# Two x tiles turned by DMA instead of on TensorE, and the k and v loads moved behind them, in a fused attention and GEGLU kernel

## The chip, the cores and the metric

The kernel runs on one core of a Trainium2 chip. The metric is the device time of one execution in microseconds (us), the median of several runs. Before the change it is 325.5 us (three runs, 325.27 to 325.55).

A core has TensorE (PE, matrix products), VectorE (DVE), ScalarE (ACT), GpSimd (POOL) and SyncE (SP), which here only issues transfers. The engines run beside each other, each works through its own instructions in program order, and they wait for one another through semaphores. The data lie in on-chip memory (SBUF); TensorE writes its results to a second memory (PSUM) of eight banks. Sixteen DMA engines move data between HBM and SBUF.

## The reference, cut to what matters

```python
# q, k, v: (8 batches, 8 heads, 576 positions, 64)
def phi(x, c, s):                       # c, s: cos and sin of the position
    r = np.maximum(x, 0.0)
    return np.concatenate([r * c, r * s], axis=-1)
q_p, k_p = phi(q, cos_w, sin_w), phi(k, cos_w, sin_w)
kv  = np.einsum('bhsf,bhsd->bhfd', k_p, v)
z   = np.sum(k_p, axis=2)
num = np.einsum('bhsf,bhfd->bhsd', q_p, kv)
den = np.einsum('bhsf,bhf->bhs', q_p, z)[..., None] + 1e-06
x   = (num / den).transpose(0, 2, 1, 3).reshape(4608, 512)

g    = x @ w_gate                       # 512 x 1536
gelu = 0.5 * g * (1.0 + erf(g / sqrt(2)))
out  = (gelu * (x @ w_val)) @ w_out     # 1536 x 512
```

Linear attention is followed by a gated feed-forward layer. Attention makes x with the tokens along the partitions; the products `x @ w_gate` and `x @ w_val` need x with its features along the partitions. Each 128 x 512 tile of x must therefore be turned. Where and when two of these tiles are turned is what the change is about.

## The kernel before

A batch has 576 tokens: four tiles of 128 and one of 64. The feed-forward layer works on blocks of tokens: block 0 is batch 0 (576 tokens), block 1 is the next 512 tokens, which are tiles 0 to 3 of batch 1, and so on. A unit (`gv_unit`) makes 128 of the 1536 hidden features of one block: four matmuls for the gate, a gelu on ScalarE, four matmuls for the value, and the product of both on VectorE. Gate results alternate between PSUM banks 0 and 1, value results between 2 and 3.

```python
def gate(n, jt, c0, w, gb, ct0=0, ct1=CT):          # TensorE, then ScalarE
    for ct in range(ct0, ct1):
        nc.tensor.matmul(ps[:, gb, 0:w], lhsT=wg_sb[:, ct, jt * 128:(jt + 1) * 128],
                         rhs=xT[:, ct, p0:p0 + w], ...)         # L232
    nc.scalar.activation(gel[:, 0:w], ps[:, gb, 0:w], AF.Gelu)  # L239
# value(): the same with wv_sb (L245), then product() on VectorE (L254)
```

The next block's attention is woven between these units. q and k are loaded as float32, scaled to bf16 by `sq` and `sk` on VectorE ("v", L136) or ScalarE ("s", L138), and v is cast to bf16:

```python
def cast_v(b, h0, h1, eng="v"):                      # L142
    cp(vx[b % 2][:, :, h0:h1, 0:D], vf[:, h0:h1].rearrange("p h j d -> p j h d"))

def kv_half(b, g, bank, eng="s", heads=None):        # 20 matmuls, L155, read kp and vx
def numer_mm(b, t, bank, g, rows=128):               # 4 matmuls, L171, read qT and kv
def norm(xb, bank, g0, g1, rows=128):                # VectorE: den, rec, then xb (L186)
```

A finished tile of x (`xb`) is turned in one of two ways. By DMA, from SyncE's queue:

```python
def turn_x(b, t, xb):
    p0 = b * S + t * 128
    xb2 = xb.rearrange("p g h d -> p (g h d)")
    if t < NJ:
        nc.sync.dma_start_transpose(out=xT[:, :, p0:p0 + 128], in_=xb2)   # L219
    ...
```

or by TensorE, with a copy from PSUM by ScalarE or VectorE:

```python
def x_by_pe(b, t, xb, bank, eng, c0=0, c1=CT):
    for ct in range(c0, c1):
        nc.tensor.transpose(out=view[:, ct, 0:rows], in_=xb2[...], identity=ident[...])  # L362
    if eng is not None:
        x_evac(b, t, bank, eng, c0, c1)              # one copy to xT, L373
```

Between block 0 and block 1 the output matmuls of block 0 (`o_part`, twelve a tile, L279; the last of them is followed by a copy on ScalarE, L309, and a store from SyncE, L311) are mixed with batch 1's attention:

```python
o_tile(0, 0, 4)
sk(NJ, 1, "s")
load_k(2)
cast_v(1, 0, 4, "v")
...
load_v(2)
o_part(0, 1, 5, 0, 6)
kv_half(1, 0, 6, "s")
kv_half(1, 1, 7, "v")
o_part(0, 1, 5, 6, 12)
y = [new_xb() for _ in range(4)]
for g in (0, 1):
    numer_mm(1, 0, 0, g)
    numer_mm(1, 1, 2, g)
norm(y[0], 0, 0, 2)
norm(y[1], 2, 0, 2)
o_part(0, 2, 4, 0, 6)
...                                  # numerator and norm of tile 2
x_by_pe(1, 0, y[0], 0, "s")
o_part(0, 2, 4, 6, 10)
x_by_pe(1, 1, y[1], 1, "s")
...                                  # numerator and norm of tile 3
o_part(0, 2, 4, 10, 12)
o_part(0, 3, 5, 0, 2)
x_by_pe(1, 2, y[2], 6, "s")
o_part(0, 3, 5, 2, 7)
x_by_pe(1, 3, y[3], 7, "s")
o_part(0, 3, 5, 7, 12)
for j in range(NJ + 1):
    sq(j, 0, "v")
sq(0, 1, "s")
```

Block 1 then starts with its units 0 to 11. For block n, `put(u, ...)` appends work behind unit u, with b = n + 1 and s = -1 for block 1 (0 for the later ones):

```python
put(2 + s, L(sk, 0, 0, "v"), L(sk, 1, 0, "v"), L(sk, 0, 1, "s"), L(sk, 1, 1, "s"))
put(3 + s, L(sk, 2, 0, "v"), L(sk, 3, 0, "v"), L(sk, 4, 0, "v"))
put(3 + s, L(sk, 2, 1, "s"), L(sk, 3, 1, "s"), L(sk, 4, 1, "s"), L(cast_v, b, 0, 4))
put(4 + s, L(cast_v, b, 4, 8, "s"))
put(5 + s, L(attn_step, b, 0))       # the two kv_half of batch b
```

Of the kernel before, what the change touches and what calls it, by code (L numbers as in the profile page):

```python
# [16 lines left out]
def kernel(  # L17
# [59 lines left out]
    def load(dst, t, b, h0=0, h1=H, even=None, odd=None, j0=0, j1=NJ + 1):  # L77
        runs = t[b, h0:h1].rearrange("h (i r) d -> i h r d", r=9)
        for s, r0, n, eng in ((1, 5, 4, odd), (0, 0, 5, even)):
            n = min(n, j1)  # L80
            (eng or nc.sync).dma_start(
                out=dst[s:128:2, h0:h1, j0:n].rearrange("p h j d -> p h (j d)"),
                in_=runs[:, :, r0 + j0:r0 + n].rearrange("i h r d -> i h (r d)"),
            )
# [55 lines left out]
    def cast_v(b, h0, h1, eng="v"):  # L140
        cp = nc.vector.tensor_copy if eng == "v" else nc.scalar.copy
        cp(vx[b % 2][:, :, h0:h1, 0:D], vf[:, h0:h1].rearrange("p h j d -> p j h d"))  # L142
# [35 lines left out]
    def norm(xb, bank, g0, g1, rows=128):  # L178

        n = g1 - g0  # L180
        nd = ps[0:rows, bank + g0:bank + g1, 0:4 * (D + 1)].rearrange("p g (h e) -> p g h e", e=D + 1)
        den = rot.tile([128, 2, 4], FP32, name="den")
        nc.vector.tensor_scalar(den[0:rows, 0:n], nd[:, :, :, D], EPS, None, op0=ALU.add)  # L183
        rec = rot.tile([128, 2, 4], FP32, name="rec")
        nc.vector.reciprocal(rec[0:rows, 0:n], den[0:rows, 0:n])
        nc.vector.tensor_tensor(  # L186
            xb[0:rows, g0:g1], nd[:, :, :, 0:D],
            rec[0:rows, 0:n, :, None].to_broadcast([rows, n, 4, D]), op=ALU.mult,
        )
# [14 lines left out]
    def new_xb():  # L204
        return rot.tile([128, 2, 4, D], BF16, name="xb", bufs=4)
# [9 lines left out]
# [5 lines that stand above are left out]
        else:  # L220
            xr = rot.tile([128, CT, 128], BF16, name="xr")
            nc.sync.dma_start_transpose(out=xr, in_=xb2)
            nc.gpsimd.tensor_copy(xT[:, :, p0:p0 + 64], xr[:, :, 0:128:2])  # L223
# [52 lines left out]
    def o_part(n, m, bank, j0, j1):  # L276
        c0 = 128 * m - starts[n] + 64
        for jt in range(j0, j1):
            nc.tensor.matmul(  # L279
                ps[:, bank, :], lhsT=hT[n % 2][:, jt, c0:c0 + 128], rhs=wo_sb[:, jt, :],  # L280
                start=(jt == 0), stop=(jt == JT - 1),
            )
        if j1 == JT:
            o_store(m, bank)
# [47 lines left out]
    def load_k(b):  # L332
        load(kf, k, b)

    def load_v(b):
        load(vf, v, b)
# [20 lines left out]
    def x_by_pe(b, t, xb, bank, eng, c0=0, c1=CT):  # L357
        xb2 = xb.rearrange("p g h d -> p (g h d)")
        rows = 128 if t < NJ else 64
        view = ps[:, bank, 0:256].bitcast(BF16).rearrange("p (c t) -> p c t", c=CT)  # L360
        for ct in range(c0, c1):
            nc.tensor.transpose(  # L362
                out=view[:, ct, 0:rows], in_=xb2[0:rows, ct * 128:(ct + 1) * 128], identity=ident[0:rows, 0:rows],
            )
        if eng is not None:
            x_evac(b, t, bank, eng, c0, c1)

    def x_evac(b, t, bank, eng, c0=0, c1=CT):
        p0 = b * S + t * 128
        cp = nc.vector.tensor_copy if eng == "v" else nc.scalar.copy  # L370
        rows = 128 if t < NJ else 64
        view = ps[:, bank, 0:256].bitcast(BF16).rearrange("p (c t) -> p c t", c=CT)
        cp(xT[:, c0:c1, p0:p0 + rows], view[:, c0:c1, 0:rows])  # L373
# [4 lines left out]
    def sk(j, which, eng, *h):  # L378
        scale(K, j, which, eng, *h)
# [110 lines left out]
    def L(f, *a):  # L490
        return lambda: f(*a)
# [24 lines left out]
        sk(j, 1, "s")  # L516
    o_tile(0, 0, 4)
    sk(NJ, 1, "s")
    load_k(2)
    cast_v(1, 0, 4, "v")  # L520
    cast_v(1, 4, 6, "v")
    cast_v(1, 6, 8, "s")
    load_v(2)
    o_part(0, 1, 5, 0, 6)
    kv_half(1, 0, 6, "s")
    kv_half(1, 1, 7, "v")
# [1 line left out]
    y = [new_xb() for _ in range(4)]  # L528
# [6 lines left out]
    for g in (0, 1):  # L535
        numer_mm(1, 2, 6, g)
    norm(y[2], 6, 0, 2)
    x_by_pe(1, 0, y[0], 0, "s")
    o_part(0, 2, 4, 6, 10)
    x_by_pe(1, 1, y[1], 1, "s")  # L540
    for g in (0, 1):
        numer_mm(1, 3, 2, g)
    norm(y[3], 2, 0, 2)
# [25 lines left out]
    for n in range(1, 7):  # L569
        b = n + 1  # L570
        a = after[n]

        def put(u, *fs):
            a[u].extend(fs)

        s = 0 if n > 1 else -1
        if n > 1:
            put(0, L(sq, 0, 0, "v"), L(sq, 1, 0, "v"), L(sq, 1, 1, "v"), L(sq, 0, 1, "s"))
            put(1, L(sq, 2, 0, "v"), L(sq, 2, 1, "s"), L(turn_q, b, 0, 3))
            put(1, L(sq, 3, 0, "v"), L(sq, 4, 0, "v"), L(sq, 4, 1, "v"), L(sq, 3, 1, "s"), L(turn_q, b, 3, 5))  # L580
        else:
            put(0, L(sq, 1, 1, "s"), L(sq, 2, 1, "v"), L(turn_q, b, 0, 3))
            put(0, L(sq, 3, 1, "v"), L(sq, 4, 1, "s"), L(turn_q, b, 3, 5))
        put(2 + s, L(sk, 0, 0, "v"), L(sk, 1, 0, "v"), L(sk, 0, 1, "s"), L(sk, 1, 1, "s"))
        put(3 + s, L(sk, 2, 0, "v"), L(sk, 3, 0, "v"), L(sk, 4, 0, "v"))
        put(3 + s, L(sk, 2, 1, "s"), L(sk, 3, 1, "s"), L(sk, 4, 1, "s"), L(cast_v, b, 0, 4))
        put(4 + s, L(cast_v, b, 4, 8, "s"))
        put(5 + s, L(attn_step, b, 0))
        if b + 1 < B:

            for f, u in zip((load_q, load_k, load_v), (3, 4, 5) if n > 1 else (1, 10, 11)):
                put(u, L(f, b + 1))
        for i in range(5):

            where = mid[n][6 + s + i] if n > 1 or i else after[n][5]
            where.append(L(attn_step, b, i + 1, 6 if n > 1 or i % 2 == 0 else 4))
# [50 lines left out]
```

## Time and profile before

| | |
|---|---|
| time, median of 3 | 325.5 us |
| span of the profiled execution | 325.0 us |
| TensorE busy | 314.3 us, 97% of the span |
| VectorE busy | 167.2 us, 51% |
| ScalarE busy | 151.9 us, 47% |
| DMA | 55.56 MB, 171 GB/s on average |
| granted TensorE clock | 0.995 of full speed |
| block 1's first gate starts on the chain | 59.67 us |
| kv of batch 2 starts on the chain | 68.30 us |

The profile lists for each engine how long it was busy. The chain of work that ended last is followed back from the last instruction, at each step to what released it; a gain or a loss on this chain is one of the whole run. The timeline lists instructions in order of time: start, length, engine, line and operation, and in brackets how long the engine had been idle and what ended that. L-numbers are lines of the kernel before. "PEld" are weight loads, which overlap the matmuls. For a transfer, the window in the timeline is that of its issue by the queue; its landing is given apart, as the time from issue until the data have arrived.

### The profile page before, as it was taken

To read this page: it belongs to the slowest core of one execution; us is meant where nothing else is said; L and a number is where in the kernel's file an instruction comes from. 1 tells how busy PE (TensorE), PEld (TensorE's weight loads), DVE (VectorE), ACT (ScalarE), POOL (GpSimd) and SP (SyncE) were. 2 spreads that over 40 slices of the span, in tenths; PEclk is the share of its full clock that TensorE was granted. 3 is DMA by queue.
4 is the path that set the end of the run, shared out by engine and by line. 5 is a ranking of instruction groups with operands and counts; after the bars stand their busy time and mean duration, and the time that the engine had idled before them with its cause. 6 is when DMAs were issued, how large, how long until landed. Compare 5 with 4: busy or idle time off the path is not lost.

```text
span 325.0 us, 5845 instructions
## 1 busy us (share of the span) xinstructions
PE 314.3 (97%) x2193; PEld 167.5 (52%) x2226; DVE 167.2 (51%) x377; ACT 151.9 (47%) x275; POOL 21.7 (7%) x43
## 2 busy tenths in 40 slices
PE   7799999999999999999999999999999999999994
PEld 2577866455445444554455445544554444444443
DVE  4785776678653676365736474547454222322210
ACT  5764665863483256425652475237622332223321
POOL 2542000001100010001000100010000100100000
PEclk9799999999999999999999999999999999999999
DMA  7999999999899929991999378965433111000024
GB/s 226 282 204 272 217 275 291 367 176 205 274 227 329 238 50 189 318 253 50 140 305 285 80 121 234 345 113 104 124 65 83 31 34 32 34 32 32 35 65 97
DMA packets 88299, 55.56 MB, mean 171 GB/s; under 512 B 53072, under 2 KB 83536, under 8 KB 88272
## 3 DMA queue, kind: packets, MB, share of 16 engines
q1 hardware_dynamic: 81744, 48.84, 60.4%
q0 software_dynamic: 6096, 5.90, 10.2%
q10 hardware_dynamic: 432, 0.46, 0.5%
q8 instruction: 17, 0.28, 0.4%
q14 instruction: 10, 0.08, 0.1%
HBM read 37.75 MB, written 9.44 MB: 145 GB/s over the span
## 4 chain that ended last, share of the span: by engine, by line
PE 90%; DMA 6%; POOL 2%; issue 1%; ACT 1%; DVE 0%; POOLq 0%; ACTq 0%
PE ps L245 28%; PE ps L279 28%; PE ps L232 28%; DMA wv_sb<-in_moe_w_val_dram 4%; PE ps L171 3%; PE ps L155 3%; DMA kf<-in_k_dram 2%; PE ps L297 1%; POOL wg_sb L326 1%; ACT kp L138 0%; POOL wv_sb L327 0%; PE ps L345 0%; PE ps L362 0%; POOL vf L99 0%; POOL qf L98 0%
## 5 line engine op out<-in xcount | busy, mean ns | idle before, releaser
L254 DVE TENSOR_TENSOR hT<-gel,ps 128x512 bf16<-128x512 f32 (+5 forms) x126 | 76.3, 608 | 91.1 <-PE ps L245 89.9
L245 PE MATMUL ps<-xT,wv_sb 128*128 128x512 bf16 (+5 forms) x496 | 112.0, 348 | 0.6
L232 PE MATMUL ps<-xT,wg_sb 128*128 128x512 bf16 (+5 forms) x492 | 111.8, 348 | 0.7
L239 ACT ACTIVATE gel<-ps 128x512 f32<-128x512 f32 (+5 forms) x126 | 67.2, 536 | 74.1 <-PE ps L232 51.5
L279 PE MATMUL ps<-wo_sb,hT 128*128 128x512 bf16 x408 | 94.3, 379 | 0.6
L232 PEld LDWEIGHTS <-wg_sb 128*128 128x128 bf16 x504 | 47.2, 98 | 44.7 <-DMA wg_sb<-in_moe_w_gate_dram 0.2
L245 PEld LDWEIGHTS <-wv_sb 128*128 128x128 bf16 x504 | 45.5, 98 | 39.4 <-DMA wv_sb<-in_moe_w_val_dram 0.5
L279 PEld LDWEIGHTS <-hT 128*128 128x128 bf16 x420 | 40.7, 98 | 47.7
L309 ACT COPY o_sb<-ps 128x512 f32<-128x512 f32 x35 | 20.5, 586 | 76.0 <-PE ps L279 69.7
L183 DVE TENSOR_SCALAR den<-ps 128x8 f32<-128x8 f32 (+1 forms) x38 | 6.3, 165 | 41.3 <-PE ps L171 41.0
L186 DVE TENSOR_TENSOR xb<-ps,rec 128x512 bf16<-128x512 f32 (+1 forms) x38 | 26.3, 691 | 2.2 <-DMA xr<-xb 0.6
L138 ACT ACTIVATE kp<-kf,sin_c 128x512 bf16<-128x512 f32 (+1 forms) x42 | 25.8, 676 | 1.2 <-DMA kf<-in_k_dram 1.2
L171 PEld LDWEIGHTS <-qT 128*128 128x128 bf16 (+1 forms) x320 | 15.4, 99 | 9.0 <-issue 0.6
L138 ACT ACTIVATE qp<-qf,sin_c 128x512 bf16<-128x512 f32 (+1 forms) x28 | 19.1, 706 | 0.0
L136 DVE TENSOR_SCALAR kp<-kf,cos_c 128x512 bf16<-128x512 f32 (+1 forms) x45 | 18.0, 451 | 1.7 <-DMA kf<-in_k_dram 1.7
L136 DVE TENSOR_SCALAR qp<-qf,cos_c 128x512 bf16<-128x512 f32 x40 | 17.6, 480 | 0.0
L171 PE MATMUL ps<-kv,qT 128*128 128x65 bf16 (+1 forms) x320 | 16.8, 195 | 0.1
L223 POOL COPY xT<-xr 128x256 bf16<-128x256 bf16 x7 | 2.8, 402 | 208.3 <-DMA xr<-xb 208.3
L155 PEld LDWEIGHTS <-kp 128*128 128x128 bf16 x320 | 11.4, 99 | 2.2 <-issue 0.6
L155 PE MATMUL ps<-vx,kp 128*128 128x65 bf16 x320 | 11.7, 196 | 0.0
L128 PE MATMUL ps<-hT 128*128 128x512 bf16 x29 | 9.1, 459 | 2.0 <-DVE par_i L105 1.7
L142 ACT CAST vx<-vf 128x1280 bf16<-128x1280 f32 (+1 forms) x9 | 9.7, 1076 | 0.7 <-DMA vf<-in_v_dram 0.7
(59 smaller groups left out, 90.6 us busy)
## 6 DMA issues: line engine op xcount, KB each, us to landing
out_dram<-o_sb SPq DMA_DIRECT2D x38, 128.0 KB, 2.4
kf<-in_k_dram SPq DMA_DIRECT2D x7, 640.0 KB, 7.1
out_dram<-o_sb SPq DMA_DIRECT2D x16, 256.0 KB, 3.0
qf<-in_q_dram SPq DMA_DIRECT2D x6, 640.0 KB, 6.0
vf<-in_v_dram SPq DMA_DIRECT2D x6, 640.0 KB, 8.7
kf<-in_k_dram SPq DMA_DIRECT2D x7, 512.0 KB, 6.1
qf<-in_q_dram SPq DMA_DIRECT2D x6, 512.0 KB, 4.7
vf<-in_v_dram SPq DMA_DIRECT2D x6, 512.0 KB, 7.7
```

What stands on the lines that cost most here:

```text
L136: nc.vector.tensor_scalar(d, s, col, 0.0, op0=ALU.mult, op1=ALU.max)
L138: nc.scalar.activation(d, s, AF.Relu, scale=col)
L142: cp(vx[b % 2][:, :, h0:h1, 0:D], vf[:, h0:h1].rearrange("p h j d -> p j h d"))
L155: nc.tensor.matmul(ps[:, bank, (h % 4) * (D + 1):(h % 4 + 1) * (D + 1)], lhsT=kp[:, j, h, :], rhs=vx[b % 2][:, j, h, 0:D + 1], start=(j == ...
L171: nc.tensor.matmul(ps[0:rows, bank + g, (h % 4) * (D + 1):(h % 4 + 1) * (D + 1)], lhsT=qT[b % 2][:, t, h, 0:rows], rhs=kv[b % 2][:, h, 0:D ...
L186: nc.vector.tensor_tensor(xb[0:rows, g0:g1], nd[:, :, :, 0:D], rec[0:rows, 0:n, :, None].to_broadcast([rows, n, 4, D]), op=ALU.mult,)
L232: nc.tensor.matmul(ps[:, gb, 0:w], lhsT=wg_sb[:, ct, jt * 128:(jt + 1) * 128], rhs=xT[:, ct, p0:p0 + w], start=(ct == 0), stop=(ct == CT - 1),
L239: nc.scalar.activation(gel[:, 0:w], ps[:, gb, 0:w], AF.Gelu)
L245: nc.tensor.matmul(ps[:, vb, 0:w], lhsT=wv_sb[:, ct, jt * 128:(jt + 1) * 128], rhs=xT[:, ct, p0:p0 + w], start=(ct == 0), stop=(ct == CT - 1),
L254: nc.vector.tensor_mul(hT[n % 2][:, jt, 64 + c0:64 + c0 + w], gel[:, 0:w], ps[:, vb, 0:w])
L279: nc.tensor.matmul(ps[:, bank, :], lhsT=hT[n % 2][:, jt, c0:c0 + 128], rhs=wo_sb[:, jt, :], start=(jt == 0), stop=(jt == JT - 1),)
L309: nc.scalar.copy(o_sb, ps[:, bank, :])
```

## The change

Tiles 0 and 1 of batch 1 are no longer turned by TensorE (four transposes and one copy on ScalarE each) but by a DMA transpose from SyncE, which takes work from TensorE. The loads of k and v of batch 2 were issued ahead of these tiles; they would now stand in front of the turns in SyncE's queue, so they are issued after both. As v then comes later, VectorE's half of the cast of v (heads 0 to 3) in block 1 moves from behind unit 2 to behind unit 3. ScalarE's half stays behind unit 3, and kv of batch 2 behind unit 4. Tiles 2 and 3 of batch 1 are still turned by TensorE.

```diff
     o_tile(0, 0, 4)
     sk(NJ, 1, "s")
-    load_k(2)
     cast_v(1, 0, 4, "v")
     cast_v(1, 4, 6, "v")
     cast_v(1, 6, 8, "s")
-    load_v(2)
     o_part(0, 1, 5, 0, 6)
...
     norm(y[2], 6, 0, 2)
-    x_by_pe(1, 0, y[0], 0, "s")
+    turn_x(1, 0, y[0])
     o_part(0, 2, 4, 6, 10)
-    x_by_pe(1, 1, y[1], 1, "s")
+
+    turn_x(1, 1, y[1])
+    load_k(2)
+    load_v(2)
...
-        put(3 + s, L(sk, 2, 1, "s"), L(sk, 3, 1, "s"), L(sk, 4, 1, "s"), L(cast_v, b, 0, 4))
+        put(3 + s, L(sk, 2, 1, "s"), L(sk, 3, 1, "s"), L(sk, 4, 1, "s"))
+        put(3 if n == 1 else 3 + s, L(cast_v, b, 0, 4))
```

In SyncE's queue the order from batch 2's q on was: q, store of output tile 0, k, v, stores of tiles 1, 2 and 3. It becomes: q, stores of tiles 0 and 1, the two turns, k, v, stores of tiles 2 and 3.

## The prediction, made before the changed kernel was run

> **What bounds the kernel now.** I read the page's busy table first, then the chain of work that ended last around the changed stretch (40 to 110 us), then the timelines of ScalarE, VectorE and SyncE there, and last the landings of single transfers.
>
> ```profile
> PE 314.3 (97%) x2193; PEld 167.5 (52%) x2226; DVE 167.2 (51%) x377; ACT 151.9 (47%) x275; POOL 21.7 (7%) x43
> ```
>
> TensorE is busy 97% of the span, and the windows of 50 to 59.67, 59.67 to 68.30 and 68.30 to 83.12 us show it idle for 0.11, 0.05 and 0.16 us. So work taken from it there shortens the run, and a wait put into it lengthens the run by as much; nothing later gives it back.
>
> The chain (start us, us, what) gives the moments that matter:
>
> ```profile
> 54.64 0.22 PE ps L362 x4
> ...
> 55.72 0.22 PE ps L362 x4
> ...
> 59.67 0.86 PE ps L232 x4
> ...
> 68.30 1.21 PE ps L155 x40
> ```
>
> L362 are the transposes that the change removes, 0.22 us of chain for four. 59.67 is the first gate of block 1, which reads four turned tiles of x, the two changed ones among them. 68.30 is kv of batch 2, the first reader of batch 2's cast v. These pieces are reckoned from the end of the matmul before; the matmuls' own records start 0.16 us earlier (59.51 and 68.14), and I use those for waits.
>
> ScalarE, then VectorE, between the two (start us, us, instruction, in brackets the idle time before it):
>
> ```profile
> 59.71 0.59 ACT L309 COPY o_sb<-ps 128x512 f32<-128x512 f32 x1 [0.49 <-PE ps L279]
> ...
> 62.99 1.33 ACT L138 ACTIVATE kp<-kf,sin_c 128x512 bf16<-128x512 f32 x2
> 64.22 0.60 ACT L239 ACTIVATE gel<-ps 128x512 f32<-128x512 f32 x1
> 64.69 1.95 ACT L138 ACTIVATE kp<-kf,sin_c 128x512 bf16<-128x512 f32 x3
> 66.53 0.60 ACT L239 ACTIVATE gel<-ps 128x512 f32<-128x512 f32 x1
> ```
>
> ```profile
> 66.75 0.95 DVE L142 CAST vx<-vf 128x1280 bf16<-128x1280 f32 x1
> 67.62 0.67 DVE L254 TENSOR_TENSOR hT<-gel,ps 128x512 bf16<-128x512 f32 x1
> 68.81 0.69 DVE L254 TENSOR_TENSOR hT<-gel,ps 128x512 bf16<-128x512 f32 x1 [0.52 <-ACT gel L239]
> ```
>
> From 59.71 on ScalarE runs without a gap (8.59 of 8.63 us busy in that window): a second chain, nearly as tight as TensorE's, and it carries the scaled k of batch 2. VectorE casts v at 66.75, before the product of unit 3 (67.62). The cast ends at 67.70, 0.44 us before kv wants it.
>
> SyncE's queue:
>
> ```profile
> 51.38 1.56 SPq L311 DMA_DIRECT2D out_dram<-o_sb  x1
> 53.03 1.39 SPq L81 DMA_DIRECT2D kf<-in_k_dram  x2
> 54.52 1.36 SPq L81 DMA_DIRECT2D vf<-in_v_dram  x2
> ```
>
> With each transfer's issue-to-landing time added to its issue, q of batch 2 lands at 56.6, the store of 51.38 at 57.3, k at 58.7 and 60.5, v at 62.0 and 63.8. Landings come in order of issue, one behind the other: 1.15 MB of k in 3.2 us, a store in about 0.6 us. The 16 engines show a share of 1.05 to 1.08 there: the transfers are a full pipe.
>
> [...] k is issued in 0.6 us and lands after 5.7 and 6.8. [...] in this stream four on TensorE hold the chain 0.22 us, and a turn of a whole 128x512 tile by DMA takes 1.2 us to issue and 2.4 to 2.6 us to land with little in front of it (the turns at 110.7 and 78.6 us). [...]
>
> **The change, part by part.**
>
> *Removed.* Eight transposes: 2 x 0.22 = **0.44 us off TensorE's chain**. Two ScalarE copies of 0.59 us (at 54.90 and 55.98) stood beside idle time of that engine and are worth nothing. All times below up to the first new wait are those of before less 0.44.
>
> *The turns.* In SyncE's new order two stores precede them. The store of tile 1 waits for its copy (52.61 + 0.59 = 53.20) and takes about 0.6 us to issue; x of tile 0 is normalised at 53.43 + 0.69 = 54.12, so the first turn is issued from about 54.2 to 55.4 and the second (its x ready at 55.16) from 55.5 to 56.7. Their data queue behind q (56.6), the first store (57.3) and the second (57.9). The turns at 71.8 and 73.5 us stood behind a q load in the same way and landed at 77.7 and 78.4, the first 0.4 us after q; so I take 0.4 to 0.6 us each: 58.4 and **58.9**. The gate of block 1 wants them at 59.51 - 0.44 = 59.07. Just in time, with 0.2 us of slack.
>
> *The loads behind them.* k is issued from 56.8. The nearest likeness is batch 3's k, issued at 81.5 and 82.2 just after the turns of batch 2: it landed after 4.3 and 5.4 us, the second at 87.6, which is 6.1 us after the first issue. So k lands at 56.8 + 6.1 = **62.9**, 2.4 us later than before. v (6.3 and 7.6 us from 82.9 and 83.5, ending at 91.1, 9.6 after k's first issue) lands at about 66.4.
>
> *ScalarE's wait.* It comes to the first scaling of k at 62.99 - 0.44 = 62.55 and waits to about 62.95: **0.4 us**. Its chain has no gap in which to recover, so the gelu of unit 3 ends at 66.53 - 0.44 + 0.60 + 0.4 = 67.09. VectorE reaches its own k scaling at 63.83 - 0.44 = 63.39 and doesn't wait.
>
> *The moved cast.* It now stands behind the product of unit 3, which needs that gelu. Product from 67.12, 0.61 us to the next start (as 61.50 to 62.11), cast 0.95 us: it ends at 68.68, and kv starts at 68.73. Without a wait for k it would be 68.33. Kv started at 68.14 before and could start at 67.70 now, so TensorE idles 1.03 us there.
>
> *Sum.* -0.44 + 1.03 = **+0.6 us**: of it +0.19 is what the moved cast costs beyond what the transposes brought, and 0.4 the wait for k.
>
> *What follows.* The turns of qp for batch 2 queue behind v (66.4) and a store (67.0). Before, they landed at 70.0 and 71.8, 4.3 us behind the stores' last landing, though they were then limited by their issue (4.27 us for the first). I put the first at 70 to 71; the numerator that reads it started at 71.33 before and is now half a microsecond later. Hidden, with little to spare.
>
> **The rivals.**
>
> 1. *A plain gain:* k lands before 62.55, and the cast hides after all. For it: TensorE is the bound, and eight instructions go. Against it: even without any wait for k, the order gelu, product, cast ends at 68.28, later than 67.70. Then 325.5 + 0.19 = 325.7; only if kv's wait were absent altogether, 325.1.
> 2. *The turns miss the gate.* SyncE took 3.7 us for a turn at 102.2 with a long queue ahead of it, and the turn landed 8.8 us after its issue. If that happened here, the gate would wait 1 to 2 us, k would come later too, and the run would be 327 to 328. Against it: at that moment a whole q, k and v were outstanding; here it is q and two stores.
> 3. *Later k hits harder:* a store takes 1.5 us to issue (as at 51.38) and not 0.6. Then k lands at 63.6 to 63.9, ScalarE waits 1.1 to 1.4 us, and the run is 326.8 to 327.1.
> 4. *Contention ahead of batch 2's qT:* its turn lands after 72, and the first numerator waits instead of, not on top of, kv. Up to 1 us more.
>
> **Range and chances.** The working gives 325.5 + 0.6 = 326.1; I lower it a little for rival 1, to 326.0. The low end is the full 0.44 us with no wait, 325.1 less a little scatter (the three times of before spread over 0.28 us); the high end is rival 3 with some of rival 2, 327.2. All of these lie within 1% of 325.5, so a change of over 2% (6.5 us) needs something that I don't see: 1% for faster, 2% for slower.
>
> **What would show it.** TensorE: L362 falls by 8 instructions; no idle time, or under 0.3 us, before the first L232 of block 1. ScalarE: a wait of 0.2 to 1 us for the DMA of kf before the first L138 of kp near 62.6. VectorE: the cast of vx after the product of unit 3, ending at 68.3 to 69.3. TensorE: about 1 us idle before the 40 matmuls of L155, released by vx. If the gate waits for xT, rival 2 holds; if kv starts at 67.7 with no gap, my order of gelu, product and cast is wrong; if a numerator waits for qT, it is rival 4.

## The result, and the profile after

The changed kernel takes **326.94 us** (median of 6 runs, 326.16 to 328.35) against 325.38 us for the kernel before, measured beside it (6 runs): a ratio of 1.0052, 95% interval 1.0031 to 1.0073. That is 1.7 us slower, with 1.0 to 2.4 us inside the interval. It lies within the predicted range and has the predicted sign, but is nearly three times the +0.6 us of the working, which lies outside the interval.

The page's busy line of the changed kernel:

```profile
PE 314.6 (97%) x2185; PEld 166.4 (51%) x2218; DVE 167.3 (51%) x377; ACT 150.8 (46%) x273; POOL 21.8 (7%) x43
```

TensorE has the eight instructions less (2193 to 2185), and no less time. Where it stands still is in its timeline, in brackets (matmul records overlap a little, so a bracket is some 0.16 us less than the lateness worked out below):

```profile
56.75 1.24 PE L279 MATMUL ps<-wo_sb,hT 128*128 128x512 bf16 x5
59.02 1.04 PE L232 MATMUL ps<-xT,wg_sb 128*128 128x512 bf16 x4 [1.02 <-DMA xT<-xb]
...
66.80 1.03 PE L245 MATMUL ps<-xT,wv_sb 128*128 128x512 bf16 x4
68.30 1.36 PE L155 MATMUL ps<-vx,kp 128*128 128x65 bf16 x40 [0.48 <-DVE vx L142]
```

There are two waits: block 1's first gate waits for the x turns, and kv of batch 2 for the cast of v. Five matmuls of L279 take 1.08 us of chain, so the gate could have started at 57.83; it started at 59.02, 1.19 us late. Four of L245 take 0.86, so kv could have started at 67.66 and came 0.64 us late. The sum -0.44 + 1.19 + 0.64 is +1.39 us. VectorE, for the second wait:

```profile
66.69 0.69 DVE L254 TENSOR_TENSOR hT<-gel,ps 128x512 bf16<-128x512 f32 x1 [0.34 <-ACT gel L239]
67.30 0.95 DVE L142 CAST vx<-vf 128x1280 bf16<-128x1280 f32 x1
```

It is the predicted order: the gelu ends, then the product, then the cast, and kv 0.05 us behind it.

**The two profiles start out of step.** The clock rows of the two pages, before and then after:

```profile
PEclk9799999999999999999999999999999999999999
```

```profile
PEclk9999999999999999999999999999999999999999
```

The profiled execution of the kernel before ran part of its second slice (8 to 16 us) at a reduced TensorE clock: 0.50 of full speed from 11.5 to 14.5 us, 0.79 over the slice, against 1.00 in the changed kernel. Its span is 325.0 us, while the spans of 57 timed runs of that kernel beside the last experiments are 322.8 to 324.4. The matmuls of L345 start at 10.25 and 10.28 us in the two, the eight of L171 behind them at 14.24 and 13.30, and at the output tiles TensorE was 1.2 us late (45.97 us, against 44.74 in the changed kernel). SyncE's transfers were not out by the same amount: q of batch 2 landed at 56.6 before and at 56.7 after, though its first part was issued at 50.0 and 48.4. So I compare a **stretch** that doesn't contain the start: from the first L279 matmul behind kv of batch 1 to the first output tile of block 1. Before, then after:

```profile
51.34 1.24 PE L279 MATMUL ps<-wo_sb,hT 128*128 128x512 bf16 x5
...
86.41 2.75 PE L279 MATMUL ps<-wo_sb,hT 128*128 128x512 bf16 x12
```

```profile
50.11 1.24 PE L279 MATMUL ps<-wo_sb,hT 128*128 128x512 bf16 x5
...
86.56 2.75 PE L279 MATMUL ps<-wo_sb,hT 128*128 128x512 bf16 x12
```

It takes 35.07 us before and 36.45 after: +1.38, the sum of the two waits less the transposes.

### The profile page after: what moved, and what is told of

The parts are those of the page before. It is cut to its first block, busy times and chain, and to the rows that moved or that the text cites. A ratio compares the mean times of both kernels' runs of the same rounds, so it can differ in the third digit from the quotient of the medians.

```text
span 325.3 us, 5831 instructions
## 1 busy us (share of the span) xinstructions
PE 314.6 (97%) x2185; PEld 166.4 (51%) x2218; DVE 167.3 (51%) x377; ACT 150.8 (46%) x273; POOL 21.8 (7%) x43
## 3 DMA queue, kind: packets, MB, share of 16 engines
q0 software_dynamic: 6096, 5.90, 10.2%
## 4 chain that ended last, share of the span: by engine, by line
PE 89%; DMA 3%; ACT 2%; DVE 2%; issue 1%; SPq 1%; POOL 0%; POOLq 0%; ACTq 0%; DVEq 0%
PE ps L232 28%; PE ps L245 27%; PE ps L279 26%; PE ps L171 3%; PE ps L155 3%; DMA vf<-in_v_dram 2%; DMA xT<-xb 1%; SPq L81 1%; ACT kp L138 1%; PE ps L297 1%; ACT gel L239 1%; PE ps L345 1%; DVE vx L142 1%; PE ps L362 0%; ACT qp L138 0%
## 5 line engine op out<-in xcount | busy, mean ns | idle before, releaser
L245 PE MATMUL ps<-xT,wv_sb 128*128 128x512 bf16 (+5 forms) x496 | 111.8, 348 | 0.4
L239 ACT ACTIVATE gel<-ps 128x512 f32<-128x512 f32 (+5 forms) x126 | 67.2, 536 | 74.9 <-PE ps L232 51.0
L279 PE MATMUL ps<-wo_sb,hT 128*128 128x512 bf16 x408 | 94.3, 379 | 0.6
L245 PEld LDWEIGHTS <-wv_sb 128*128 128x128 bf16 x504 | 45.6, 98 | 39.0
L279 PEld LDWEIGHTS <-hT 128*128 128x128 bf16 x420 | 40.7, 98 | 47.7
L171 PEld LDWEIGHTS <-qT 128*128 128x128 bf16 (+1 forms) x320 | 15.2, 98 | 9.1 <-issue 0.3
L171 PE MATMUL ps<-kv,qT 128*128 128x65 bf16 (+1 forms) x320 | 16.6, 194 | 0.2
L128 PE MATMUL ps<-hT 128*128 128x512 bf16 x29 | 10.0, 503 | 1.8 <-DVE par_i L105 1.7
```

The costliest lines, as they stand in the source:

```text
L171: nc.tensor.matmul(ps[0:rows, bank + g, (h % 4) * (D + 1):(h % 4 + 1) * (D + 1)], lhsT=qT[b % 2][:, t, h, 0:rows], rhs=kv[b % 2][:, h, 0:D ...
L245: nc.tensor.matmul(ps[:, vb, 0:w], lhsT=wv_sb[:, ct, jt * 128:(jt + 1) * 128], rhs=xT[:, ct, p0:p0 + w], start=(ct == 0), stop=(ct == CT - 1),
L279: nc.tensor.matmul(ps[:, bank, :], lhsT=hT[n % 2][:, jt, c0:c0 + 128], rhs=wo_sb[:, jt, :], start=(jt == 0), stop=(jt == JT - 1),)
```

## The experiments

All ratios are to the kernel before. Stretch differences come from one profile each, and say which part of a difference arises in the changed part.

| kernel | ratio (95%) | stretch, us over before | TensorE waits in it |
|---|---|---|---|
| changed kernel | 1.0052 (1.0031 to 1.0073) | +1.38 | gate for xT, kv for vx |
| changed, cast back | 1.0033 (1.0020 to 1.0045) | +0.95 | gate (0.19), numerator for qT |
| cast moved only | 1.0024 (1.0014 to 1.0035) | +0.63 | kv |
| cast and loads moved, no turns | 1.0017 (1.0009 to 1.0024) | +0.64 | kv |
| the same with spare turns | 1.0053 (1.0040 to 1.0066) | +1.39 | kv |
| turns behind k and v | 1.0274 (1.0254 to 1.0295) | +9.01 | gate |
| stores 0, 1 behind k and v | 1.0083 (1.0063 to 1.0104) | +2.36 | kv, numerator |
| the same, cast back | 1.0113 (1.0098 to 1.0129) | +4.12 | numerator |
| stores 0 to 3 behind qT | 1.0058 (1.0038 to 1.0078) | +1.72 | kv, a value of unit 10 |
| the same, cast back | 1.0047 (1.0031 to 1.0063) | +1.57 | a value of unit 10 |
| stores 2, 3 late, cast back | 1.0027 (1.0017 to 1.0037) | +1.00 | gate (see there) |
| before, stores 2, 3 late | 1.0015 (1.0008 to 1.0021) | 0.00 | none |
| all four stores late, cast back | 1.0010 (0.9997 to 1.0024) | -0.32 | none (one behind it) |

The last but one is a control and a caution: no wait and the same stretch, yet measured 0.5 us slower. Only about 0.2 us of it lie between the first and the last instruction (median spans of the timed runs 323.5 and 323.25 us); the rest lies outside what the profile shows. Differences of that size between two programs arise outside the stretch too, and I don't explain them by it.

### The cast, alone and taken back

```diff
# cast only: the kernel before with
+        put(3 if n == 1 else 3 + s, L(cast_v, b, 0, 4))   # was behind unit 2
```

> The kernel before with nothing but the cast moved behind unit 3. Both theories: the order gelu, product, cast makes TensorE wait for vx ahead of kv, 0.5 to 0.65 us, ratio 1.0015 to 1.002. A third theory C (the cast hides, and its cost in the changed kernel is only a lateness of k or v): no wait ahead of kv, ratio 1.000. Its trace is also a second look at block 0 of an unchanged queue: theory B wants the q load to land at 56.5 to 57 us whether TensorE is early or late.

Measured: ratio 1.0024, stretch +0.63 us. TensorE's timeline of it:

```profile
67.14 1.36 PE L155 MATMUL ps<-vx,kp 128*128 128x65 bf16 x40 [0.47 <-DVE vx L142]
```

With k and v early and x turned by TensorE, the order alone makes kv wait. This part of the prediction (+0.19 beyond the 0.44 us of the transposes, so 0.63) holds. Theory B's guess about the queue doesn't: it wanted q of batch 2 to land at 56.5 to 57 us, and here it landed at 55.2.

> The changed kernel with VectorE's half of the cast of v back behind unit 2. Theory A (the prediction's: the loss comes from the moved cast and the wait for k, and the turns reach the gate in time): the 0.6 us of idle time before kv goes, and the run is 0.2 to 0.44 us faster than the kernel before (ratio 0.9987 to 0.9995). Theory B (the turns' landing is set by the transfers queued ahead of them, and block 1's first gate waits about 1 us for them in a normal execution): the idle time before kv goes, the wait of the gate for xT stays at about 1 us, and the run is 0.5 to 0.7 us slower than the kernel before (ratio 1.0015 to 1.0022).

Measured: ratio 1.0033, stretch +0.95. The wait ahead of kv goes; the gate waits 0.19 us in this execution; and a wait comes up that neither theory named, in TensorE's timeline:

```profile
56.69 1.24 PE L279 MATMUL ps<-wo_sb,hT 128*128 128x512 bf16 x5
58.12 1.04 PE L232 MATMUL ps<-xT,wg_sb 128*128 128x512 bf16 x4 [0.19 <-DMA xT<-xb]
...
69.09 1.02 PE L245 MATMUL ps<-xT,wv_sb 128*128 128x512 bf16 x4
70.96 0.43 PE L171 MATMUL ps<-kv,qT 128*128 128x65 bf16 x8 [0.84 <-DMA qT<-qp]
```

The first numerator of batch 2 waits for the turn of its q, which landed 9.6 us after its issue at 61.4. Theory A is out (the run is slower than before, not faster), and theory B is incomplete: the gate is only 0.35 us late (58.12 against 56.69 + 1.08), and yet the ratio is above the 1.0022 that theory B allows. Up to the gate this program is the changed kernel's, in which the gate was 1.19 us late: in one execution q of batch 2 landed at 55.8 and in the other at 56.7, though issued within 0.1 us of each other. So the 0.43 us of stretch between the two isn't the cast's alone, and the intervals of their ratios overlap.

### The stores, behind k and v: both theories wrong

```diff
+        if m in (0, 1):                 # in o_store
+            held.append(lambda: nc.sync.dma_start(out=rows_ap(128 * m, 128), in_=o_sb))
...
     load_v(2)
+    for f in held:
+        f()
```

> The changed kernel with the stores of output tiles 0 and 1 (256 KB each) issued behind the loads of k and v instead of ahead of the turns. Theory B: about 1.2 us less in front of the turns, they land at about 57.8 us, the wait of the gate shrinks from 1.0 us to 0 to 0.2, the idle time before kv stays at about 0.6 us: ratio to before 1.0000 to 1.0010, 1.0 to 1.3 us below the changed kernel. Theory A: the turns were in time anyway, only the wait for k (0.2 to 0.4 us) goes, 0.4 us below the changed kernel, ratio about 1.004.

> Both edits: the two stores behind k and v, and the cast back behind unit 2. Theory B: neither the gate nor kv waits, and what is left is the gain of eight transposes: 0.3 to 0.5 us faster than before, ratio 0.9985 to 0.9991. Theory A: the same, 0.3 to 0.44 us. If it is not faster than before, a wait is left that neither theory names.

Measured: ratios 1.0083 and 1.0113, worse than the changed kernel. The turns do reach the gate (they land at 55.6 and 56.1 us in the first). But SyncE's timeline of the first shows a hole and a jam:

```profile
48.13 1.31 SPq L81 DMA_DIRECT2D qf<-in_q_dram  x2
52.13 2.51 SPq L219 DMA_TRANSPOSE xT<-xb  x2
54.74 1.30 SPq L81 DMA_DIRECT2D kf<-in_k_dram  x2
...
60.29 10.71 SPq L146 DMA_TRANSPOSE qT<-qp  x2
```

Between q (issue ended at 49.44) and the first turn, which waits for x, SyncE issues nothing for 2.7 us. From 50 to 60 us the 16 DMA engines show a share of 0.94, against 1.16 in the changed kernel, and from the landing of q to that of the last store ahead of the turn of q it takes 12.2 us, against 10.2. The stores that stood in this gap now stand ahead of the turn of q, whose first issue takes 7.75 us (4.27 before) and which lands at 71.6. TensorE:

```profile
71.65 0.43 PE L171 MATMUL ps<-kv,qT 128*128 128x65 bf16 x8 [1.56 <-DMA qT<-qp]
```

In the second kernel it waits longer, and then runs slowly:

```profile
71.95 0.62 PE L171 MATMUL ps<-kv,qT 128*128 128x65 bf16 x8 [2.57 <-DMA qT<-qp]
72.38 1.90 PE L232 MATMUL ps<-xT,wg_sb 128*128 128x512 bf16 x4
```

Four such matmuls take 1.03 us elsewhere. The earlier arrival at the wait (no kv wait ahead of it) makes the wait longer: the 2.57 us are about the sum of the two waits of the first kernel, 0.91 ahead of kv and 1.56 here. What comes on top is the clock, 0.50 of full speed from 72 to 75.2 us, which makes about 1.6 us (an estimate: half of 3.2). So taking the cast back is a loss here.

From these runs came **theory C**: SyncE's queue is a second chain, from q of batch 2 to the last turns for block 2. What the change puts into it comes out as a wait somewhere, at the gate, at kv (through k) or at the numerator (through qT).

### The turns as transfers, without and with dependants

```diff
# no turns: the changed kernel with
-    turn_x(1, 0, y[0])
+    x_by_pe(1, 0, y[0], 0, "s")        # and the same for tile 1
# spare turns: that, with at the same places
+    xs0 = rot.tile([128, CT, 128], BF16, name="xr")
+    nc.sync.dma_start_transpose(out=xs0, in_=y[0].rearrange("p g h d -> p (g h d)"))
```

> The changed kernel with tiles 0 and 1 turned by TensorE again: cast and loads stay moved. Theory C (formed on the first four runs: the queue of transfers from q of batch 2 to the turn of batch 2's q is a second chain; the two turns and the gaps that they leave in it make that last turn land later, and the first numerator of batch 2 waits for it): without the turns k and v come about 1 us or more earlier than in the changed kernel, the turn of q lands in time, and only the wait ahead of kv is left, perhaps lengthened by k or v coming after the store of tile 1: ratio to before 1.002 to 1.003, less than the 1.0052 of the changed kernel. Theory D (the loads' later place alone is what hurts, the turns are harmless): ratio as of the changed kernel, 1.005.

> The changed kernel with tiles 0 and 1 turned by TensorE again, and the two DMA turns kept at their place in the queue, writing a spare tile that nobody reads (work added: these two turns). Their cost as transfers alone, with no gate that depends on them and no gain on TensorE. Theory C (the two turns lengthen the queue that ends in the turn of batch 2's q, for which the first numerators wait): 0.7 to 1.6 us slower than the same kernel without them (ratio 1.0017), so ratio 1.004 to 1.0065, with a wait of a numerator for qT or of ScalarE for kf in its trace. Theory E (the turns cost only through the gate that waits for them): ratio as without them, 1.0015 to 1.002, and no wait for qT.

Measured: 1.0017 without turns, 1.0053 with spare ones; stretches +0.64 and +1.39. Theories D and E fall. The later place of the loads costs nothing by itself (+0.64 against +0.63 with the cast alone), and two turns that feed nothing cost 0.75 us of stretch (1.2 us of time by the ratios). ScalarE of the kernel with spare turns, then TensorE:

```profile
62.49 1.33 ACT L138 ACTIVATE kp<-kf,sin_c 128x512 bf16<-128x512 f32 x2 [0.66 <-DMA kf<-in_k_dram]
```

```profile
68.27 1.36 PE L155 MATMUL ps<-vx,kp 128*128 128x65 bf16 x40 [1.23 <-DVE vx L142]
```

k is complete at 62.4 us with spare turns and at 60.1 without turns. ScalarE waits for it, gelu, product and cast follow, and kv pays. I had expected a wait for qT or for kf; it was kf, and qT, landing at 71.1, just came in time behind it. The changed kernel also has k at 62.4, but there the gate has already held TensorE and ScalarE, so ScalarE hardly waits:

```profile
61.88 0.60 ACT L239 ACTIVATE gel<-ps 128x512 f32<-128x512 f32 x1
62.53 1.33 ACT L138 ACTIVATE kp<-kf,sin_c 128x512 bf16<-128x512 f32 x2
```

In the profile of before both scalings of k start 0.47 us behind their gelu (62.52 to 62.99, 64.22 to 64.69), here the first starts 0.65 behind. That the two sums are so near (+1.38 and +1.39) is partly chance. Counted from the landing of q, k is complete after 4.8 us without turns, 5.7 in the changed kernel (5.8 with the cast back) and 6.7 with spare turns: the turns that feed the gate put k off by about 1 us, the spare ones by 1.9, and why the spare ones cost more stays open. The changed kernel has k as late only because its q landed 1.0 us later.

> The kernel before with the two turns by DMA and nothing else: loads and cast at their old places, so the turns stand behind k and v in the queue. All theories that take the queue for first in, first out: the turns land half a microsecond after v, at 63 to 64 us, the gate (57.7) waits 5 to 6 us, ratio 1.015 to 1.022[...]. If the transfers overtook each other, it would be under 1.005.

Measured: 1.0274, stretch +9.01. TensorE:

```profile
63.73 1.87 PE L232 MATMUL ps<-xT,wg_sb 128*128 128x512 bf16 x4 [6.45 <-DMA xT<-xb]
```

The gate waited 6.45 us for turns that stood behind k and v, somewhat more than the 5 to 6 us expected of a queue worked off first in, first out; this is why the change moves the loads. The loss is more than the wait: from 62.7 to 69.5 us the granted clock was 0.50, and the four matmuls above took 1.87 us.

### Clearing the queue

> The changed kernel with the stores of output tiles 0 to 3 (four of 256 KB) issued behind the turn of batch 2's q, and the cast back behind unit 2. Theory C: with no stores ahead of it the turn of q lands 4.3 us behind v (at about 64.5), so at 68.5 to 69.5, in time for the first numerator at 69.2; the x turns land at about 56, before the gate; nothing waits, and the eight transposes are a gain at last: ratio 0.9985 to 0.9992. Theory D: k and v are as late as in the two runs with the stores behind k and v (ratios 1.008 and 1.011), and the run stays above 1.005.

> The same with the cast left behind unit 3. Theory C: only the wait ahead of kv stays (0.5 to 0.9 us) and the numerator doesn't wait: ratio 1.0005 to 1.002. Theory D: above 1.005.

Measured: 1.0047 and 1.0058, not the gain of theory C and, with the cast left behind, above the 1.005 of theory D. There kv is 1.3 us late, more than theory C's 0.5 to 0.9: k landed at 61.4 after ScalarE had stood idle for 0.5 us, so theory D is right about k. Gate and numerator no longer wait: qT lands at 67.7 and 67.5. The jam moved on: the stores and batch 3's q now stand ahead of the turns for block 2. VectorE and TensorE of the first:

```profile
79.02 0.69 DVE L186 TENSOR_TENSOR xb<-ps,rec 128x512 bf16<-128x512 f32 x1 [3.75 <-DMA xr<-xb]
```

```profile
80.35 1.02 PE L245 MATMUL ps<-xT,wv_sb 128*128 128x512 bf16 x4 [1.82 <-DVE hT L254]
```

A new x tile needs the buffer that the turn of batch 1's last tile is still reading; VectorE waits with the products behind it, and TensorE for them.

> The changed kernel with the cast back behind unit 2 and the stores of output tiles 2 and 3 (256 KB each) issued only behind the last x turn of batch 2. Theory C: the turn of q lands 1.2 us earlier than with the cast back alone (ratio 1.0033), no numerator waits, the later turns are not pushed back either; what is left is the wait of the gate for the x turns, 0.2 to 1.0 us, against 0.44 us gained: ratio 0.999 to 1.002. Theory E: the stores don't matter, ratio 1.0025 to 1.0045.

> The kernel before with the same two stores issued late and nothing else: the control. Theory C: before has about a microsecond of slack at the numerator, so nothing is gained, ratio 0.999 to 1.0005. If it is clearly faster, the queue already costs the kernel before some time, and a gain of the run with turns would be that of the stores.

Measured: 1.0027 and 1.0015. In the first neither kv nor a numerator waits; the gate does:

```profile
58.83 1.04 PE L232 MATMUL ps<-xT,wg_sb 128*128 128x512 bf16 x4 [1.27 <-ACT qp L138]
```

The bracket names ScalarE's first scaling of q, which ended at 58.80. But in the changed kernel the gate starts (59.02) before that instruction ends (59.24), so it doesn't need it. I read the wait as one for the turns, which landed at 58.4 and 58.8 us behind a q that landed at 56.4. The stretch is +1.00, and the ratio is above the range of theory C and within that of theory E (here: the stores don't matter). By the ratio alone the two can't be told apart from each other; the trace shows no wait for qT, as theory C foretold, and a gate that waits longer than with the cast back. The control shows an unchanged stretch, but its ratio is above the 1.0005 that I gave as the most.

```diff
# the last one: all four stores held; tiles 0 and 1 behind the last x turn
# of batch 2, tiles 2 and 3 behind batch 3's v
+        if n == 1:
+            put(9, *held[0:2])
+            put(11, *held[2:4])
```

> The changed kernel with the cast back behind unit 2 and all four stores of output tiles 0 to 3 taken out of the crowded stretch: tiles 0 and 1 stored behind the last x turn of batch 2, tiles 2 and 3 behind the load of batch 3's v. Theory C: the x turns reach the gate (landing about 56.5, gate at 57.5), the turn of q lands at about 68 and batch 1's last turn at about 75, nothing in the stretch waits, and from kv of batch 1 to the first output tile of block 1 the trace shows 36.1 us, against 36.56 for the kernel before and 37.93 for the changed one. The time then is about 0.4 us under before by that; the control with two late stores measured 0.5 us over before with the same 36.55 us of stretch, so a ratio of 0.9980 to 1.0005 is what this theory allows. If a wait is left in the stretch, its releaser says which transfer is still late, and theory C is incomplete. Theory E: as with the cast back alone, ratio 1.0025 to 1.0045.

Measured: 325.53 us (22 runs, 324.38 to 328.71), ratio 1.0010, interval 0.9997 to 1.0024: not told apart from the kernel before. The ratio is above theory C's 1.0005, with an interval that reaches into its range, and below theory E's. In the stretch the theory holds: no wait, 34.75 us, 0.32 less than before where 0.44 was to be had. The page has the same clock row as before, with the 7 in the second slice, and TensorE came late to the gate (58.26); the turns, landed at 56.7 and 57.1, would have been in time for a gate at 57.5 too. In the profiled execution the jam came back behind the stretch, at the gate of block 3:

```profile
117.07 1.02 PE L232 MATMUL ps<-xT,wg_sb 128*128 128x512 bf16 x4 [1.53 <-DMA xT<-xb]
```

Seven of the 22 runs lie below 325.0 us and four above 326.5; the profiled one (327.37) is one of the four, and whether the other three had this wait I can't tell. No kernel here beats the one before beyond doubt.

## Why the prediction was right, and where it was not

**Right:** 0.44 us of chain for eight transposes (from the first L279 of the stretch to where the gate could start it takes 8.17 us before and 7.72 after). The turns' landing behind q: 2.3 us foretold, 2.3 measured, and 2.3 to 2.4 in three more kernels with both stores ahead of them. The cost of the moved cast, in the run with the cast alone. No numerator waited in the profiled execution (rival 4), though that wait is real: it appeared as soon as the cast was taken back. (One reading was off and nothing rests on it: the turn at 78.6 us took 1.5 us to issue, not 1.2.)

**Right by luck:** the landing of the second turn to 0.1 us (58.9 foretold, 59.0 measured) and k's (62.9 and 62.4). They start from q at 56.6 in one execution, and q happened to land at 56.7 in the other; with the cast back it landed at 55.8 and the turn at 58.1. Lucky, too, is the range: with its working alone the prediction misses the interval, and the measured 326.94 us lies in it because its high end allowed for "rival 3 with some of rival 2". Rival 3 didn't come (the store of tile 1 took 0.57 us to issue); rival 2 did.

**The step that failed is the one of the turns, "just in time, with 0.2 us of slack".** The gate waited for them and started 1.19 us late, where the working has no wait. The queue was as long as foretold; what was wrong is to take the moment of the gate and that of q from one execution as fixed to each other to 0.2 us. The kernel with the cast moved alone is that of before up to there, and has the gate in TensorE's timeline at

```profile
57.88 1.03 PE L232 MATMUL ps<-xT,wg_sb 128*128 128x512 bf16 x4
```

with q landed at 55.2. From q to the gate this is 2.7 us; in the profile of before it is 2.9, and in the control with two late stores 1.8 (57.91 after 56.1). Less the 0.44 us of the transposes, the turns' 2.3 us would have fitted with 0.2 us to spare before, and been short by up to 1.0 in the others. In the kernels with turns and both stores ahead of them the gate could have started 1.2 us (changed), 2.0 (cast back) and 1.0 (stores 2 and 3 late) after q, and came 1.19, 0.35 and 1.44 late. In the profile of before TensorE was 1.2 us late at the output tiles, behind the stretch at 0.50 of full clock, which flatters the slack; why q lands now earlier and now later against TensorE stays open. Rival 2 named this wait, and I dismissed it by an argument about the length of the queue; the length was as I said, and the wait came all the same.

**The term that was mis-sized is ScalarE's wait for k**, 0.4 us predicted, as good as nothing measured. From the gate to kv it takes 9.28 us in the changed kernel and 9.26 with the cast moved alone, so the 0.64 us ahead of kv are the cast's. Its scaling of k does come 0.18 us later behind its gelu, but the gate's wait had given ScalarE that time. In place of -0.44 + 0.63 + 0.4 stands -0.44 + 1.19 + 0.64.

**Not in the working at all** was what the two turns do to the transfers behind k and v. From the last landing of q to that of the first turn of qp it takes 13.5 us without turns, and 15.1 and 15.4 in the kernels with the cast back and with spare turns. In the profiled execution of the changed kernel it was 12.9: there that turn landed 2.7 us behind the store ahead of it, in the other three 4.2 to 4.3. Why stays open, and so whether a numerator waits in other executions of the changed kernel. Open also is the last 0.3 us between the stretch (+1.38) and the ratio (+1.7), which is inside the ratio's interval.

## What to carry to other kernels

With the transfers as crowded as here (a DMA share of 1.16 from 50 to 60 us in the changed kernel), reordering didn't make the wait disappear: the orders tried moved it from the gate to the numerator (0.84 to 2.57 us), to a buffer (3.75 us on VectorE) and to a later block (1.53 us), and only taking all four stores out of the crowded stretch removed it from there. Before you trust a slack between an engine and a transfer, look at it in more than one execution, and compare the span and clock row of the profile with the timed runs: 0.2 us is worth nothing where the distance between the landing of q and the gate varied by 1.1 us between three executions with the same work up to there. And a transpose moved from a full TensorE to a full queue has to be charged there: here two turned tiles freed 0.44 us of TensorE's chain, and the two turns as spare transfers cost 0.75 us of stretch.

## What the runs showed of the hardware

- The granted TensorE clock was 0.50 of full speed from 11.5 to 14.5 us before (a matmul at 10.25 had waited 2.28 us for qp), from 72 to 75.2 us with stores 0 and 1 behind k and v and the cast back (a wait of 2.57 us had ended at 71.95) and from 62.7 to 69.5 us with the turns behind k and v (a wait of 6.45 us ended at 63.73). In the last two, four matmuls behind the wait took 1.90 and 1.87 us instead of 1.03. In the changed kernel the early matmul waited 0.65 us, and the clock was 1.00 from 8 to 16 us. Whether the waits caused the lower clock these runs don't show.
- The two turns of 128x512 bf16 tiles (0.13 MB each) landed about 0.5 us apart (58.4 and 59.0 us in the changed kernel, 55.6 and 56.1 with stores 0 and 1 behind k and v); two stores of 256 KB, twice the bytes, landed about 0.6 us apart (66.3 and 66.9 in the changed kernel). Two turns put off the completion of a k load behind them by about 1 us where they fed the gate and by 1.9 us as spare ones, counted from the landing of q.
- The issue of the first turn of q on SyncE took 4.27 us before, 5.28 in the changed kernel, 6.32 with the cast back and 7.75 with stores 0 and 1 behind k and v. It ended after the last transfer ahead of it had landed: at 67.0 after 65.7 before, at 67.5 after 66.9 in the changed kernel, at 68.0 after 67.2 with the stores behind k and v. The second turn of q was issued only then, at 67.2 before and 67.7 in the changed kernel. What held the issue up the traces don't show.
